# Decay-table rows spread over every sixteenth partition, and earlier products of zeros, in a fused RetNet and feed-forward kernel

**Chip, cores, metric.** One Trainium2 chip, one core. Times are device microseconds (us) of that core. Executions are compared with executions of the other kernel on the same chip.

## The reference

```python
# q, k, v: (4, 8, 768, 64); w_in: (512, 2048); w_out: (2048, 512); all f32
gamma = 1.0 - 2.0 ** (-5.0 - np.arange(H))
for t in range(S):
    state = gamma[None, :, None, None] * state + einsum('bhd,bhe->bhde', k[:, :, t], v[:, :, t])
    y[:, :, t] = scale * einsum('bhd,bhde->bhe', q[:, :, t], state)
x = y.transpose(0, 2, 1, 3).reshape(B * S, H * D)
h = x @ w_in
out = np.maximum(0.01 * h, h) @ w_out
```

The kernel does the recurrence in chunks of 128 tokens (scores, mask, products with the values, state) and the feed-forward part with seven block products in place of eight. Powers of the decay are needed per head and position; they come from a host-made table of 8 rows of 780 numbers, which three small matmuls spread over the 128 partitions.

## The kernel before

The change touches only the opening. In order of the program (cuts marked by `...`):

```python
x, t = xs[0]
rows = t[0:H, 1:3].rearrange("p i k n -> p (i k n)")[:, 0 : decay.shape[1]]
nc.scalar.dma_start(out=rows, in_=decay)         # the table: 8 rows, partitions 0 to 7
load_qk(0, 0); load_v(0, 0); load_qk(0, 1); ...  # SyncE's queue: all other loads
nc.vector.memset(mask, 1.0)
nc.gpsimd.affine_select(out=mask, ...)
...
nothing = t[:, 0, 0, :].bitcast(BF16)            # zeros, in the table's tile, other columns
nc.vector.memset(t[:, 0, 0, :], 0.0)

def keep_busy(n):                                # products of zeros
    for _ in range(n):
        nc.tensor.matmul(idle..., lhsT=nothing[:, 0:128], rhs=nothing, ...)
...
keep_busy(7)
score(0, 0)
nc.tensor.matmul(tables[:, 0, 0:H], lhsT=by_head, rhs=ones, ...)         # from the table
nc.tensor.matmul(tables[:, 0, H : H + HP], lhsT=place, rhs=g_c, ...)
masked(0, 0)
nc.vector.tensor_copy(out=dec[:, n_gq:], in_=tables[:, 0, 0 : H + HP])
nc.tensor.matmul(spread..., lhsT=place, rhs=g_q, ...)
nc.scalar.copy(out=dec[:, 0:n_gq], in_=spread...)
decay_v(0, 0, nc.vector)
score(0, 1)
values(0, 0)
```

## Time and profile before

| | before |
|---|---|
| median of 6 executions | 668.31 us (666.85 to 670.25) |
| profiled execution | 666.64 us, span 664.9 us |
| TensorE busy in the span | 659.4 us |
| first product of zeros / first scores / second scores start | 1.40 / 4.63 / 7.81 us |
| full clock from (the trace's record of the granted clock) | 6.01 us |
| first matmul of the hidden layer | 13.93 us |

A line of the timeline gives start, duration, engine, line, operation, written and read tile, number of records; in brackets the idle time before it and what ended that. `ap` are scores, `tables` and `spread` the products that make decay tables, `idle` the products of zeros, `d` the first hidden-layer products.

### The profile page before, as it was taken

To read this page: it belongs to the slowest core of one execution; us is meant where nothing else is said; L and a number is where in the kernel's file an instruction comes from. 1 tells how busy PE (TensorE), PEld (TensorE's weight loads), DVE (VectorE), ACT (ScalarE), POOL (GpSimd) and SP (SyncE) were. 2 spreads that over 40 slices of the span, in tenths; PEclk is the share of its full clock that TensorE was granted. 3 is DMA by queue.
4 is the path that set the end of the run, shared out by engine and by line. 5 is a ranking of instruction groups with operands and counts; after the bars stand their busy time and mean duration, and the time that the engine had idled before them with its cause. 6 is when DMAs were issued, how large, how long until landed. Compare 5 with 4: busy or idle time off the path is not lost.

```text
span 664.9 us, 10405 instructions
## 1 busy us (share of the span) xinstructions
PE 659.4 (99%) x4505; PEld 573.6 (86%) x4505; DVE 373.9 (56%) x570; ACT 175.8 (26%) x322; POOL 20.1 (3%) x22
## 2 busy tenths in 40 slices
PE   8999999999999999999999999999999999999998
PEld 5888888888888888888888888888888888888886
DVE  5789969889888676325543613663431444431342
ACT  5854555264261002212201311210221220221210
POOL 0000000000000111001000100100100000000000
PEclk9999999999999999999999999999999999999999
DMA  8920312313222453003012100301300001000001
GB/s 327 403 97 33 126 64 79 112 65 113 109 85 75 166 184 127 1 1 128 1 46 81 64 1 1 127 1 64 128 1 0 2 0 45 19 1 1 0 1 63
DMA packets 15758, 48.92 MB, mean 74 GB/s; under 512 B 1753, under 2 KB 2009, under 8 KB 15713
## 3 DMA queue, kind: packets, MB, share of 16 engines
q1 hardware_dynamic: 15696, 48.24, 20.1%
q8 instruction: 35, 0.57, 0.3%
q14 instruction: 11, 0.08, 0.0%
q10 hardware_dynamic: 16, 0.02, 0.0%
HBM read 41.97 MB, written 6.29 MB: 73 GB/s over the span
## 4 chain that ended last, share of the span: by engine, by line
PE 99%; DMA 1%; DVE 0%; issue 0%
PE B_o L414 13%; PE A_o L414 13%; PE C_o L414 12%; PE C_h L414 12%; PE B_h L414 12%; PE A_h L414 12%; PE D_o L414 6%; PE D_h L414 6%; PE ap L165 4%; PE yp L193 4%; PE d L436 2%; PE yp L184 2%; PE yp L208 1%; DMA qk<-in_qk_dram 1%; PE sums L208 0%; PE idle L626 0%
## 5 line engine op out<-in xcount | busy, mean ns | idle before, releaser
L414 PE MATMUL A_h<-x,w 128*128 128x256 f32 x368 | 87.0, 379 | 0.0
L414 PEld LDWEIGHTS A_h<-x,w 128*128 128x128 f32 x368 | 69.9, 190 | 9.6 <-issue 0.2
L414 PE MATMUL A_o<-g,w 128*128 128x256 f32 x288 | 68.0, 379 | 0.0
L449 ACT ACTIVATE g<-g 128x512 f32<-128x512 f32 x69 | 42.0, 630 | 92.4 <-DVE g L361 92.4
L414 PEld LDWEIGHTS A_o<-g,w 128*128 128x128 f32 x288 | 54.8, 190 | 7.4
L454 ACT COPY m<-A_h 128x512 f32<-128x512 f32 x23 | 13.4, 582 | 143.6 <-PE A_h L414 103.9
L361 DVE TENSOR_TENSOR m<-m,B_h 128x512 f32<-128x512 f32 x23 | 15.8, 686 | 55.5 <-PE B_h L414 55.5
L361 DVE TENSOR_TENSOR m<-m,B_o 128x512 f32<-128x512 f32 x16 | 11.0, 685 | 63.9 <-PE B_o L414 63.9
L238 DVE TENSOR_TENSOR x<-yp,dec 128x512 f32<-128x512 f32 x24 | 16.4, 689 | 49.7 <-PE yp L208 35.6
L414 PE MATMUL C_h<-t,w 128*128 128x256 f32 x184 | 44.1, 383 | 0.0
L414 PE MATMUL B_h<-x,w 128*128 128x256 f32 x184 | 44.1, 383 | 0.0
L414 PE MATMUL B_h<-t,w 128*128 128x256 f32 x184 | 43.5, 379 | 0.0
L414 PE MATMUL D_h<-t,w 128*128 128x256 f32 x184 | 43.5, 379 | 0.0
L414 PE MATMUL C_h<-x,w 128*128 128x256 f32 x184 | 43.5, 379 | 0.0
L414 PEld LDWEIGHTS C_h<-t,w 128*128 128x128 f32 x184 | 34.5, 190 | 5.5 <-issue 0.9
L414 PEld LDWEIGHTS B_h<-t,w 128*128 128x128 f32 x184 | 35.0, 190 | 4.7
L414 PEld LDWEIGHTS D_h<-t,w 128*128 128x128 f32 x184 | 35.0, 190 | 4.7
L414 PEld LDWEIGHTS C_h<-x,w 128*128 128x128 f32 x184 | 35.0, 190 | 4.7
L414 PEld LDWEIGHTS B_h<-x,w 128*128 128x128 f32 x184 | 34.5, 190 | 5.0 <-issue 0.3
L364 DVE TENSOR_TENSOR gd<-g,gd 128x512 f32<-128x512 f32 x48 | 37.1, 773 | 1.7
L170 DVE TENSOR_TENSOR am<-ap,mask 128x1024 f32<-128x1024 f32 x24 | 28.5, 1220 | 10.8 <-PE ap L165 10.8
L414 PE MATMUL B_o<-gd,w 128*128 128x256 f32 x144 | 34.0, 379 | 0.0
(118 smaller groups left out, 1019.0 us busy)
## 6 DMA issues: line engine op xcount, KB each, us to landing
raw<-in_weights_dram SPq DMA_DIRECT2D x31, 512.0 KB, 4.3
qk<-in_qk_dram SPq DMA_DIRECT2D x19, 512.0 KB, 3.8
kv<-in_kv_dram SPq DMA_DIRECT2D x17, 512.0 KB, 4.4
out_dram<-o SPq DMA_DIRECT2D x23, 256.0 KB, 2.1
in<-in_qk_dram SPq DMA_DIRECT2D x3, 512.0 KB, 8.7
in<-in_kv_dram SPq DMA_DIRECT2D x3, 512.0 KB, 8.5
kv<-in_kv_dram SPq DMA_DIRECT2D x4, 256.0 KB, 7.0
o_in<-in_qk_dram SPq DMA_DIRECT2D x2, 512.0 KB, 8.6
```

The costliest lines, as they stand in the source:

```text
L165: nc.tensor.matmul(ps[ts(u, 64), j, a, :], lhsT=x[ts(j, 64), 1, a, ts(u, 64)], rhs=x[ts(j, 64), 0, a, :])
L170: nc.vector.tensor_tensor(out=am.rearrange("p j a t -> p (j a) t"), in0=scores[c, b].rearrange("p j a t -> p (j a) t"), in1=mask.unsqueeze ...
L184: nc.tensor.matmul(ps[ts(i, 64), j, m, :], lhsT=st[b][ts(j, 64), a, :], rhs=x[ts(j, 64), 0, a, :], start=(m == 0), stop=False, skip_group_ ...
L193: nc.tensor.matmul(ps[ts(i, 64), j, m, :], lhsT=y[:, 1, 2 * a + j, :], rhs=am[:, j, a, :], start=(c == 0 and m == 0), stop=True, skip_grou ...
L208: nc.tensor.matmul(sp[ts(j, 64), a, :], lhsT=y[:, 0, 2 * a + j, :], rhs=y[:, 1, 2 * a + j, :], start=start, stop=True, skip_group_check=True)
L238: nc.vector.tensor_tensor(out=blocks, in0=ps[:, :, 0 : HP // 2, :], in1=gq, op=ALU.mult)
L361: nc.vector.tensor_tensor(out=out, in0=a, in1=b, op=ALU.add)
L364: nc.vector.tensor_tensor(out=out, in0=a, in1=b, op=ALU.subtract)
L414: nc.tensor.matmul(half, lhsT=block(w, sa)[:, k, ts(i, 128)], rhs=rhs[:, k, :], start=(first and (i == 0 or split) and n == 0 and k == 0), ...
L436: nc.tensor.matmul(banks[r][:, i, :], lhsT=block(2 * u, r + 2 * kh)[:, k, ts(i, 128)], rhs=x[:, 2 * kh + th, k, :], start=(step == 0 and i ...
L449: nc.scalar.activation(g[:, i], g[:, i], AF.Prelu, alpha=0.01)
L454: nc.scalar.copy(out=got["m1"], in_=ps)
```

## The change

Its intent: let the tables' products use the array's full height (rows in partitions 0, 16, 32, ... with zeros between), start the products of zeros sooner, and take two small pieces of work off VectorE.

```diff
-    rows = t[0:H, 1:3].rearrange("p i k n -> p (i k n)")[:, 0 : decay.shape[1]]
-    nc.scalar.dma_start(out=rows, in_=decay)
+    rows = t[:, 1:3].rearrange("p i k n -> p (i k n)")[:, 0 : decay.shape[1]]
+    nothing = t[:, 0, 0, 0:64].bitcast(BF16)
+    nc.vector.memset(t[:, 0, 0, 0:64], 0.0)
+    half = decay.shape[1] // 2
+    nc.gpsimd.memset(rows[:, :half], 0.0)
+    nc.vector.memset(rows[:, half:], 0.0)
+    nc.scalar.dma_start(out=rows[0 : 128 : 128 // H], in_=decay)
...
-    nothing = t[:, 0, 0, :].bitcast(BF16)
-    nc.vector.memset(t[:, 0, 0, :], 0.0)
...
-            nc.tensor.matmul(idle.rearrange("p i n -> p (i n)"), lhsT=nothing[:, 0:128],
-                             rhs=nothing, start=True, stop=True, skip_group_check=True)
+            nc.tensor.matmul(idle.rearrange("p i (two n) -> p (i two) n", two=2), lhsT=nothing,
+                             rhs=nothing.unsqueeze(1).to_broadcast([128, 4, 128]),
+                             start=True, stop=True, skip_group_check=True)
...
-    keep_busy(7)
+    keep_busy(8)
...
-    nc.vector.tensor_copy(out=dec[:, n_gq:], in_=tables[:, 0, 0 : H + HP])
+    nc.scalar.copy(out=dec[:, n_gq:], in_=tables[:, 0, 0 : H + HP])
...
-    decay_v(0, 0, nc.vector)
+    decay_v(0, 0)
```

## The prediction

> **What bounds the kernel now.** I read the page first, then the chain that ended last over the first 46 us, then the timeline of the first 15 us, because every line of the diff is executed in the opening. From the page:
>
> ```profile
> PE 659.4 (99%) x4505; PEld 573.6 (86%) x4505; DVE 373.9 (56%) x570; ACT 175.8 (26%) x322; POOL 20.1 (3%) x22
> PE 99%; DMA 1%; DVE 0%; issue 0%
> ```
>
> TensorE is busy for 659.4 of 664.9 us, so 5.5 us is all that removing its waits could give. The changed kernel has the same matmuls in the same order after the opening, so what it saves must come from TensorE's waits or its slow stretches before about 14 us. The chain by time shows that opening:
>
> ```profile
> 0.80 3.78 DMA qk<-in_qk_dram
> 4.59 0.04 issue
> 4.63 1.75 PE ap L165 x32
> 6.38 0.31 PE tables L638 x2
> 6.69 0.22 PE tables L640 x2
> 6.91 0.96 PE spread L644 x2
> 7.88 1.03 PE ap L165 x32
> 8.91 1.02 PE yp L193 x16
> ...
> 11.48 0.70 DVE x L238
> 12.18 0.05 issue
> 12.23 1.10 PE ap L165 x32
> 13.34 0.75 PE idle L626 x3
> 14.09 3.45 PE d L436 x16
> ```
>
> The first scores wait for the first transfer (4.59 us), whatever TensorE does before. The same 32 score records take 1.75 us the first time and 1.03 to 1.10 us later: their first six groups of four start 0.21 us apart, the later ones half of that. So TensorE runs at half rate until about 6.0 us, which agrees with the trace's record of the clock: full from 6.01 us. The slow stretch costs 1.75 - 1.10 = 0.65 us here. The timeline has the rest:
>
> ```profile
> 0.80 0.58 ACTq L592 DMA_DIRECT2D t<-decay_dram  x1
> 0.90 0.17 DVE L609 MEMSET mask<- 128x128 f32 x1 [0.90 <-PEq L836]
> 1.07 0.27 DVE L621 MEMSET t<- 128x256 f32 x1
> 1.40 3.17 PE L626 MATMUL idle<-t 128*128 128x512 bf16 x7 [1.40 <-DVE t L621]
> 7.67 0.16 DVE L643 COPY dec<-tables 128x12 f32<-128x12 f32 x1
> 7.87 0.69 DVE L147 TENSOR_TENSOR kv<-kv,dec 128x512 f32<-128x512 f32 x1
> 8.39 1.07 POOL L147 TENSOR_TENSOR kv<-kv,dec 128x512 f32<-128x512 f32 x1 [6.96 <-DMA kv<-in_kv_dram]
> 8.98 1.23 DVE L170 TENSOR_TENSOR am<-ap,mask 128x1024 f32<-128x1024 f32 x1 [0.42 <-PE ap L165]
> ```
>
> The products of zeros exist only to keep TensorE active; they start at 1.40, when VectorE has cleared their operand.
>
> **What the Trainium skill says.** "TensorE: Matmul & The Clock Gate", Part 1: TensorE starts at 1.2 GHz and is let up to 2.4 GHz after a sustained busy window of about 3.4 us; the window runs free of the kernel's start, so the moment varies from run to run. The trace agrees on the rates: the idle products' weight loads are 0.425 us apart (512 columns at 1.2 GHz), and the later products of the same form take about 0.21. Its full clock came 6.01 - 1.40 = 4.61 us after the first product, between one and two windows. The same page, "LDWEIGHTS (loading the stationary operand)": a load's time goes by columns, not by rows of contraction. The trace agrees: 187 ns for the 8-row loads of the tables, 190 ns for 128-row loads of f32. So full-height tables cost TensorE no more time. "SBUF — State Buffer", "SBUF: two separate sides": VectorE and GpSimd exclude each other only where VectorE uses the shared port pair, for example with two operands in SBUF. The masking reads PSUM and one SBUF operand; it took 1.23 us with GpSimd at work beside it (8.98) and 1.22 to 1.23 elsewhere, so a second GpSimd product does not slow it.
>
> **The change part by part.**
> 1. *Zeros sooner.* The memset of 64 columns is now VectorE's first. From 0.17 us for 128 columns and 0.27 for 256, a column costs 0.78 ns and the fixed part is 0.07 us: 64 columns take 0.12 us. TensorE starts at 0.90 + 0.12 + 0.05 (the lag seen before) = 1.07 instead of 1.40, so 0.33 us sooner. Eight products fill 8 x 0.425 = 3.40 us, to 4.47; seven from 1.40 filled to 4.38. Both end before the transfer at 4.59, so the eighth costs nothing. What is gained is an earlier window: on average 0.33 us less at half rate. Where that stretch falls on work, it is worth half, some 0.16 us.
> 2. *Clearing before the transfer.* The table's transfer now waits for two memsets of 390 columns. VectorE's takes 0.07 + 390 x 0.78 ns = 0.37 us and is done at 1.40. For GpSimd I have only its 128-column select of 0.29 us, so at worst 0.9 us from 0.8, done at 1.7. The issue moves from 0.80 to between 1.45 and 1.75. In the trace its eight packets of 3,120 B were all done by 2.43, 1.63 us after the issue; now that is 3.1 to 3.4, perhaps 4 because it shares the engines with the first load. The tables are wanted at about 6. Off the path. The 24 KB now run beside the 512 KB of the first scores' load: 5% of it, at most about 0.1 us on the 4.59.
> 3. *Full-height tables.* The same four pairs of records, the same columns: 0 us of TensorE time. Its effect can only be on how activity is counted (rival A).
> 4. *Copy to ScalarE, first decay to GpSimd.* VectorE loses 0.16 + 0.69 = 0.85 us of work, but then waits for the second scores, which end at 8.91: its next masking stays at 8.98. On the other side, the 12-column copy need no longer wait behind the masking (6.53 to 7.76): ScalarE does it at about 6.95 to 7.2, GpSimd's product takes 1.07 us, done at about 8.3; the products with the values want it at 8.84. GpSimd is free again before the second values land (8.39). Nothing gained, nothing lost.
> 5. *How much of an earlier TensorE reaches the end.* In the trace the second scores' load had landed at 7.59 and they began at 7.81, 0.07 before the modelled end of the table product, which is how TensorE passes from group to group: TensorE was the bound, by about 0.2 us. The third scores began at 12.23; their load landed at 12.10, and the tile before was taken at 12.17. So of any gain, about 0.1 us survives to 12.2 when the clock comes as in this trace. Sum: 0.33 x 0.5 = 0.16, capped at about 0.1, less up to 0.1 for the shared transfer: 0 to 0.1 us of 668.
>
> **The rivals.**
> A. *The window is missed in many runs of before.* If eight-row products hardly count as activity, a window that holds the tables (6.3 to 7.8) fails and the full clock comes 3.4 us later, which costs up to 3.4 x 0.5 = 1.7 us of work. For it: the profiled execution took 666.64, while the median is 668.31 and the slowest 670.25; the first step is 1.67 us. Full-height rows and an earlier start would bring most runs to 666.5 to 667. Against it: the one trace shows no missed window, and the spread can have other causes, such as the transfers that run near 400 GB/s from 5 to 25 us.
> B. *The transfers bound the opening anyway.* For it: landing and need lie within 0.2 us at both 7.8 and 12.2, and the queue is saturated. The time would stay at 668.0 to 668.4.
> C. *A new wait takes the old one's place.* If GpSimd's memset or the shared queue makes the table late, the tables stand in TensorE's order ahead of the second scores, and every tenth is lost directly; if GpSimd's first decay comes late, so do the values' products. Against it: slack of 2 us on the first, 0.5 us on the second. It would make 669 to 670.
>
> **Range and chances.** I weigh A at 0.4 with 666.9, B and the bare sum at 0.45 with 668.2, C at 0.15 with 669.2: 0.4 x 666.9 + 0.45 x 668.2 + 0.15 x 669.2 = 667.8. The range, 666.4 to 669.3, is wider than the sum because three runs of the kernel before already span 3.4 us. A change of 2% is 13.4 us, the whole opening, so the chances of that are token: faster 0.01, same 0.98, slower 0.01.
>
> **What would show each step right or wrong.** Step 1: the first idle product at about 1.07 and eight of them, the scores still at about 4.6. Step 2: the table product never waits for its transfer. Step 3: the table loads still at about 187 ns, now of 128 rows. Step 4: the copy on ScalarE near 7.0, GpSimd's first decay done before 8.5, VectorE's second masking within 0.2 us of 8.98. Step 5: third scores no earlier than about 12.1 and the chain from 14 us on unchanged. A: the full clock's start spread by one window or more between executions of before and not of after, and after's times tighter. I am wrong if the opening up to the first hidden-layer product (13.9 us) moves by over 1 us without a change of clock, if anything after 46 us changes, or if the median leaves the range.

## The result, and the profile after

The changed kernel took 672.74 us (median of 6, 671.79 to 673.46) against 668.31: ratio 1.0063, 95% interval 1.0041 to 1.0086. That is within 2%, but clearly slower, and above the predicted range of 666.4 to 669.3. A ratio here and below is the mean time of one kernel's fast executions over that of the other's of the same rounds, so not quite the ratio of the medians. A repetition beside the experiments gave 672.29 us, ratio 1.0073 (1.0058 to 1.0088).

The busy line of the page of the changed kernel shows the same TensorE work in a span of 670.4 us:

```profile
PE 659.3 (98%) x4506; PEld 572.5 (85%) x4506; DVE 371.6 (55%) x569; ACT 175.7 (26%) x323; POOL 21.1 (3%) x24
```

So 5.5 us of waiting were added between these two executions (that of before, 666.64 us, was among its fastest; the medians differ by 4.4). Where: busy times by stretch, first the kernel before, then the changed one (stretch, its length, then busy us of each engine with instructions, the clock, the DMA share and GB/s).

```profile
0.00:5.00 5.00, 3.54 (x15) 1.26 (x19) 0.44 (x2) 1.28 (x1) 0.50 (x5) 1.00 0.52 174
5.00:10.00 5.00, 5.00 (x87) 3.69 (x79) 3.01 (x4) 1.04 (x2) 1.07 (x1) 1.00 0.96 378
```

```profile
0.00:5.00 5.00, 0.00 (x0) 0.00 (x0) 0.64 (x3) 1.28 (x1) 0.92 (x6) 1.00 0.58 181
5.00:10.00 5.00, 2.55 (x7) 0.93 (x8) 0.00 (x0) 0.00 (x0) 0.00 (x0) 1.00 1.01 398
```

TensorE did nothing in the first 5 us. The 1.00 in the clock's column does not show the start: the record begins only where the full clock does. The timeline of the changed kernel tells what TensorE waited for:

```profile
0.89 0.11 DVE L593 MEMSET t<- 128x64 f32 x1 [0.89 <-PEq L841]
...
1.50 1.17 ACTq L597 DMA_DIRECT2D t<-decay_dram  x1
...
7.45 3.44 PE L629 MATMUL idle<-t 128*128 128x512 bf16 x8 [7.45 <-DMA t<-decay_dram]
```

VectorE has the zeros ready at 1.00 us, but the products of zeros start at 7.45, released by the table's transfer, although they read no column of the table. In the trace two waits for semaphores (counters that tell an engine when another has finished) stand before the first product: an instruction of the products' own line waits for the semaphore of the table's transfer, then the first weight load waits for VectorE's. In the kernel before, there is VectorE's alone. The memsets of the rows (VectorE 1.03 to 1.41, GpSimd 0.80 to 1.22) come ahead of that transfer, which is issued at 1.50 instead of 0.80 and needs 5.81 us instead of some 2 until it lands, that is, until its last completion is recorded. (SyncE's next load of weights also waits 1.9 us for that landing and is issued at 7.33 instead of 5.55; the chain to the end contains no transfer but the table's.) The chain of the changed kernel (start, duration, what):

```profile
1.50 5.81 DMA t<-decay_dram
...
7.45 3.44 PE idle L629 x8
10.89 1.03 PE ap L165 x32
...
13.42 1.03 PE ap L165 x32
...
19.17 3.86 PE d L436 x16
```

The eight products of zeros, which used to fill a wait, now stand on the path: the first scores start at 10.82 instead of 4.63, although their load had landed at 4.6. The first hidden-layer product is at 19.17 instead of 13.93, and the 5.24 us between are nearly the whole 5.5. The scores now run at full rate (1.10 instead of 1.75 us), which gives 0.65 of the 6.19 us back.

### The profile page after: what moved, and what is told of

The parts are those of the page before. It is cut to its first block, busy times and chain, and to the rows that moved or that the text cites. A ratio compares the mean times of both kernels' runs of the same rounds, so it can differ in the third digit from the quotient of the medians.

```text
span 670.4 us, 10409 instructions
## 1 busy us (share of the span) xinstructions
PE 659.3 (98%) x4506; PEld 572.5 (85%) x4506; DVE 371.6 (55%) x569; ACT 175.7 (26%) x323; POOL 21.1 (3%) x24
## 4 chain that ended last, share of the span: by engine, by line
PE 98%; DMA 1%; DVE 0%; issue 0%; DVEq 0%
PE B_o L414 12%; PE A_o L414 12%; PE C_o L414 12%; PE C_h L414 12%; PE B_h L414 12%; PE A_h L414 12%; PE D_o L414 6%; PE D_h L414 6%; PE yp L193 3%; PE ap L165 3%; PE d L436 2%; PE yp L184 2%; PE yp L208 1%; DMA t<-decay_dram 1%; PE idle L629 1%; PE sums L208 0%
## 5 line engine op out<-in xcount | busy, mean ns | idle before, releaser
L364 DVE TENSOR_TENSOR gd<-g,gd 128x512 f32<-128x512 f32 x48 | 35.4, 737 | 1.7
L147 POOL TENSOR_TENSOR kv<-kv,dec 128x512 f32<-128x512 f32 x18 | 20.2, 1125 | 463.3 <-DMA kv<-in_kv_dram 258.8
```

Source lines behind the costliest of these rows:

```text
L147: engine.tensor_tensor(out=v, in0=v, in1=gk.unsqueeze(2).to_broadcast([128, H, D]), op=ALU.mult)
L364: nc.vector.tensor_tensor(out=out, in0=a, in1=b, op=ALU.subtract)
```

## The experiments

Theory W: the wait of the products of zeros for the table costs the time. Rivals: L, the late table alone costs it; M, the moves to ScalarE and GpSimd cost it. Of each kernel six executions were compared with eleven of the kernel before on the same chip.

| run | median (us) | range (us) | ratio to before, 95% |
|---|---|---|---|
| a1 changed, again | 672.29 | 671.85 to 672.73 | 1.0073, 1.0058 to 1.0088 |
| e1 zeros in another tile | 668.41 | 667.56 to 671.02 | 1.0026, 1.0005 to 1.0048 |
| e2 rows together | 667.10 | 666.66 to 667.77 | 1.0001, 0.9984 to 1.0017 |
| e2 again | 666.87 | 666.65 to 667.00 | 0.9990, 0.9975 to 1.0005 |
| e3 before, table late | 668.87 | 666.38 to 670.66 | 1.0020, 0.9994 to 1.0045 |
| e4 no zeros | 670.24 | 669.68 to 670.67 | 1.0045, 1.0030 to 1.0060 |
| e5 moves only | 667.64 | 667.06 to 670.28 | 1.0009, 0.9988 to 1.0029 |
| e6 e1, table second in queue | 667.52 | 666.92 to 667.89 | 1.0003, 0.9988 to 1.0019 |
| e7 wait kept, table early | 671.31 | 670.78 to 671.74 | 1.0058, 1.0043 to 1.0072 |
| e8 e6 with 8 rows | 667.47 | 666.84 to 668.98 | 1.0000, 0.9982 to 1.0018 |
| e9 e1, wait filled | 668.17 | 667.46 to 668.73 | 1.0009, 0.9993 to 1.0024 |

The kernel before had medians of 666.95 or 666.96 on these chips.

**a1: the changed kernel once more**, on the chip of e3, e5 and e7; no edit.

> The changed kernel unaltered, on the chip of this job, to have it beside the experiments. 1.005 to 1.009 of the kernel before, first product of zeros again at 7 to 7.5 us, none of its runs as short as the kernel before.

As expected: the slowdown is there again, and the first product of zeros is at 7.10 us:

```profile
7.10 3.57 PE L629 MATMUL idle<-t 128*128 128x512 bf16 x8 [7.10 <-DMA t<-decay_dram]
```

**e1: the changed kernel without the false wait.**

```diff
-    nothing = t[:, 0, 0, 0:64].bitcast(BF16)
-    nc.vector.memset(t[:, 0, 0, 0:64], 0.0)
+    parts = [new_g(0, 0)]                  # moved up; its difference tile is not used yet
+    zeros = parts[0][2][:, 0, 0, 0:64]
+    nothing = zeros.bitcast(BF16)
+    nc.vector.memset(zeros, 0.0)
```

> The changed kernel with the zeros in another tile, so that the products of zeros no longer wait for the table's transfer; all else as changed. Theory W (that wait is the cost): first product of zeros at 1.1 us instead of 7.4, first scores at 4.6; the tables then still wait for a transfer that lands near 7.3, so the second scores start near 8.8 instead of 7.8 (before) or 13.4 (changed); about 668.0 to 669.5 us. Rival L (the late table, not the wait, is the cost): zeros early, but the time stays within 1 us of the changed kernel's 672.7. Rival M (the moves to ScalarE and GpSimd cost it): also stays near 672.7.

Most of the loss is gone. Timeline of e1, profiled in an execution of 669.13 us:

```profile
1.05 3.22 PE L630 MATMUL idle<-gd 128*128 128x512 bf16 x8 [1.05 <-DVE gd L595]
...
6.95 0.36 PE L644 MATMUL tables<-t 128*128 128x8 f32 x2 [1.23 <-DMA t<-decay_dram]
...
7.59 2.05 PE L650 MATMUL spread<-t 128*128 128x512 f32 x2
...
9.58 1.57 PE L165 MATMUL ap<-qk 64*64 64x128 f32 x32
```

Zeros at 1.05 and, in the same view, first scores at 4.62, as W expected. The tables then wait 1.23 us for the transfer, and `spread` takes 2.05 us instead of 1.10: the clock fell. The record of the clock says full from 3.76, half from 7.18, full again from 10.59 us. The second scores start at 9.58, later than the 8.8 expected, for this reason. Of the six executions three took 667.6 to 667.7 and three 669.1 to 671.0. The recorded clock of the three slow ones, as a mean over the span, is 0.997, 0.995 and 0.995, that of the others 0.999 to 1.000; one window of 3.41 us at half rate is 0.003 of the span, so the slow ones fell for one or two windows.

**e2: rows together in partitions 0 to 7, no clearing, transfer at once; zeros sooner and moves kept.**

```diff
-    rows = t[:, 1:3].rearrange("p i k n -> p (i k n)")[:, 0 : decay.shape[1]]
+    rows = t[0:H, 1:3].rearrange("p i k n -> p (i k n)")[:, 0 : decay.shape[1]]
-    half = decay.shape[1] // 2
-    nc.gpsimd.memset(rows[:, :half], 0.0)
-    nc.vector.memset(rows[:, half:], 0.0)
-    nc.scalar.dma_start(out=rows[0 : 128 : 128 // H], in_=decay)
+    nc.scalar.dma_start(out=rows, in_=decay)
```

> The changed kernel with the table's eight rows in partitions 0 to 7 as before, without the clearing, so its transfer is issued at 0.8 us and nothing else waits for it; the zeros sooner and the moves to ScalarE and GpSimd stay. Theories W and L both: transfer landed by 2.5 us, first product of zeros at 1.1, opening as before or up to 0.3 us sooner, 667 to 668.5 us. Rival M (the moves cost it): stays above 671.

As expected, but for the landing at 2.67 us instead of by 2.5, for which nothing waits. Timeline of e2:

```profile
1.05 3.59 PE L626 MATMUL idle<-t 128*128 128x512 bf16 x8 [1.05 <-DVE t L593]
...
6.41 0.17 ACT L645 COPY dec<-tables 128x12 f32<-128x12 f32 x1 [3.73 <-PE tables L642]
6.67 1.04 POOL L147 TENSOR_TENSOR kv<-kv,dec 128x512 f32<-128x512 f32 x1 [5.16 <-ACT dec L645]
```

The zeros lie in the table's tile here too, and the trace has no wait for the transfer before them. Nor has e3 below, which keeps the clearing (of 8 rows) and not the stride: the wait comes with the strided rows. That the framework's tracking takes a destination of every sixteenth partition as covering the columns between is inferred from the waits in these traces; its code was not read. Rival M falls: with both moves in place GpSimd's product is done at 7.71, well before the values' products.

**e4: the changed kernel without the first products of zeros**.

```diff
-    keep_busy(8)
+    keep_busy(0)
     score(0, 0)
```

> The changed kernel without the first eight products of zeros, so nothing stands before the first scores; the late table stays. Theory W: the first scores start at 4.6 us at half rate, the tables wait for the transfer to land near 7.3, the clock stays low until about 8 to 12 us; 3 to 4.5 us faster than the changed kernel, 668.2 to 669.7, so that the products meant to help cost more than they give. Rival L: within 1 us of 672.7.

Timeline of e4, first scores, `spread` and second scores:

```profile
4.81 1.98 PE L165 MATMUL ap<-qk 64*64 64x128 f32 x32 [4.81 <-DMA qk<-in_qk_dram]
...
8.15 2.05 PE L649 MATMUL spread<-t 128*128 128x512 f32 x2
...
10.13 1.99 PE L165 MATMUL ap<-qk 64*64 64x128 f32 x32
```

The scores start at 4.81 and the tables wait for the transfer until 7.30, but the full clock comes only at 12.25 us, so tables and second scores take nearly twice their time. The gain over the changed kernel is 0.0073 - 0.0045 = 0.0028, some 1.9 us, less than the 3 to 4.5 expected: dropping the products saves their place on the path and loses the clock.

**e6: e1 with the table's transfer second in SyncE's queue.**

```diff
-    nc.scalar.dma_start(out=rows[0 : 128 : 128 // H], in_=decay)
     load_qk(0, 0)
+    nc.sync.dma_start(out=rows[0 : 128 : 128 // H], in_=decay)
```

> As e1_zeros_own_tile, and the table's transfer is issued on SyncE's queue right after the first scores' load, ahead of all others, instead of on ScalarE's queue. Theory W with the table queued behind other loads: landed between 4.0 and 5.5 us instead of 7.3, the tables don't wait, second scores at 7.7 to 8.1; 667 to 668.5 us, 0.5 to 1 below e1. If the strided rows themselves make the transfer slow: lands near 7 as before and no faster than e1. If full-height tables matter for the clock: tighter times than the kernel before, mean below 667.5.

Timeline of e6, the table's issue, the tables and the second scores (the first scores start at 4.38):

```profile
1.50 0.72 SPq L600 DMA_DIRECT2D t<-decay_dram  x1
...
5.42 0.39 PE L644 MATMUL tables<-t 128*128 128x8 f32 x2
...
7.84 1.10 PE L165 MATMUL ap<-qk 64*64 64x128 f32 x32 [0.85 <-DMA qk<-in_qk_dram]
```

The table's last completion is recorded at 5.04 us, the tables wait for nothing, and the kernel is level with before. So full height itself shows no cost (the interval allows up to 0.2%) and no gain in the times of six executions: none was below 666.9.

**e7: the wait kept, the table early** (e6's queue, zeros in the table's tile as changed; against the changed kernel).

```diff
-    nc.scalar.dma_start(out=rows[0 : 128 : 128 // H], in_=decay)
     load_qk(0, 0)
+    nc.sync.dma_start(out=rows[0 : 128 : 128 // H], in_=decay)
```

> A smaller dose of the same wait: the zeros stay in the table's tile, so the products of zeros wait for its transfer, but that is issued second in SyncE's queue and lands near 4 us (it did in e6). Theory W: first product of zeros near 4.2 us, eight of them take 3.4 us, first scores at 7.6 to 7.8 instead of 4.4 (e6) and 10.8 (changed), 1.5 to 3 us above e6, so 1.002 to 1.005 of the kernel before. If the wait did not matter (rival L), as e6, 1.000.

Chain of e7:

```profile
1.50 3.93 DMA t<-decay_dram
...
5.57 3.57 PE idle L629 x8
```

The transfer landed at 5.43, not near 4: I had taken the packets' start in e6 for their landing. So the loss against e6 is also larger than the 1.5 to 3 us expected. The zeros start at 5.57, 4.5 us after e6's 1.05, and the ratio is 0.0055 above e6, 3.7 us. In a1 they start at 7.10, 6.05 us after e6's, and the ratio is 0.0070 above it, 4.7 us. Both are about 0.8 us of time for each us that the zeros wait: the cost follows the dose (in a1 the table's queue differs from e6's as well), and rival L, which expected e7 to equal e6, falls.

**e3: the kernel before with only the memsets ahead of the table's transfer.**

```diff
+    nc.gpsimd.memset(rows[:, :half], 0.0)      # rows: partitions 0 to 7
+    nc.vector.memset(rows[:, half:], 0.0)
     nc.scalar.dma_start(out=rows, in_=decay)
```

> The kernel before with its eight rows in partitions 0 to 7, and only the two memsets ahead of the table's transfer, so that it is issued near 1.5 to 2 us behind the other loads: late table alone, no stride, no false wait. If being late in the queue is the cause of the late landing: lands at 6.5 to 7.5 us as in the changed kernel and in e1, the tables wait until then, 1.001 to 1.004 of the kernel before, and in some runs the clock falls while TensorE waits. If the stride over partitions were the cause: lands by 4 us, 1.000.

A miss with a lesson. The issue took 0.58 us at 1.42, the last completion is at 5.25 us, between the two forecasts, and the tables did not wait. Yet three executions took 670.6 and three 666.4 to 667.2. The profiled one is a slow one, its full clock came at 14.36 us, and TensorE's timeline shows what comes before it at half rate, scores in 1.99 and `spread` in 2.05 us:

```profile
1.80 3.17 PE L629 MATMUL idle<-t 128*128 128x512 bf16 x7 [1.80 <-DVE t L624]
4.90 1.99 PE L165 MATMUL ap<-qk 64*64 64x128 f32 x32
...
7.69 2.05 PE L647 MATMUL spread<-t 8*128 8x512 f32 x2
```

The memset of the zeros came third on VectorE, so the products of zeros started 0.4 us later than before (1.80, not 1.40). Nothing else that TensorE waits for had moved, so this is the likely cause that three of six executions, and not five of 39, fell into the slow group. The trace supports it: counted back from 14.36 in steps of 3.413 us (the spacing of the clock's changes in e1, e5 and e8), a window ends at 4.12, of which products of zeros from 1.80 on fill 2.32 us. TensorE was busy for 2.66 us of the window after which e5 got the full clock, and for 2.71 us of e1's.

**e9: e1 with the wait filled.** Five more products of zeros after the first scores.

```diff
     keep_busy(8)
     score(0, 0)
+    keep_busy(5)
```

> As e1_zeros_own_tile (strided rows, late table, no false wait) with five more products of zeros after the first scores, which fill the wait for the table. If half of e1's runs were slow because the clock fell in that wait: no fall in the trace, six runs between 667.2 and 668.3, ratio 1.001 to 1.002 that is left for the wait itself. If the clock had no part in it: the same two groups of times as e1 (667.6 and 669 to 671).

Timeline of TensorE in e9:

```profile
6.26 1.25 PE L630 MATMUL idle<-gd 128*128 128x512 bf16 x5
7.92 0.36 PE L645 MATMUL tables<-t 128*128 128x8 f32 x2 [0.41 <-DMA t<-decay_dram]
...
8.36 1.10 PE L651 MATMUL spread<-t 128*128 128x512 f32 x2
```

The transfer landed later still here (7.79 us), yet the clock stayed full from 5.95 us on, `spread` kept its 1.10 us, and no execution exceeded 668.73 (668.3 was expected). The recorded clock of all six is 0.999 to 1.000. e1's slow group is gone. Six executions without it could be chance, but the recorded clock of e1's own executions says the same: a falling clock made the slow ones slow.

**e5: the moves alone**, in the kernel before (the last two pairs of lines of the change's diff).

> The kernel before with only the 12-column copy on ScalarE and the first decay product on GpSimd. Theories W and L: no change, 0.999 to 1.001. Rival M (a slower engine becomes the wait): the products with the values start later than 8.84 us and 1.001 to 1.005.

Timeline of TensorE in e5:

```profile
6.25 1.10 PE L644 MATMUL spread<-t 8*128 8x512 f32 x2
7.29 1.86 PE L165 MATMUL ap<-qk 64*64 64x128 f32 x32
```

The ratio's interval includes 1. The profiled execution (667.68 us) had its clock fall from 7.47 to 10.89 us, so the second scores took 1.86 us and the products with the values came at 9.08, later than the 8.84 that rival M named as its sign. They stand right behind those scores, though, and e2, with the same moves and no fall, has them at 8.52. The run does not speak for M; a loss of up to 0.3% by the moves alone is not excluded by it.

**e8: e6 with the eight rows together**, to test the height of the tables' products at the same timing.

```diff
-    rows = t[:, 1:3].rearrange("p i k n -> p (i k n)")[:, 0 : decay.shape[1]]
+    rows = t[0:H, 1:3].rearrange("p i k n -> p (i k n)")[:, 0 : decay.shape[1]]
...
-    nc.sync.dma_start(out=rows[0 : 128 : 128 // H], in_=decay)
+    nc.sync.dma_start(out=rows, in_=decay)
```

> As e6_table_second_in_queue but with the eight rows together in partitions 0 to 7 (the memsets stay ahead of the transfer), so that only the height of the tables' products and the stride of the transfer differ from e6. If products of 8 rows count less than full ones for the clock: the trace or some of the six runs show a fall or a late start of the full clock, runs some 1.5 to 3.5 us above the best, where e6 had none. If not: as e6, 667.0 to 668.0 in all runs. The issue should take near 0.4 us instead of 0.72 if the stride makes it longer, and the table land at or before 5.0 us.

Two of six executions took 668.8 and 669.0, and the trace of one shows the clock falling from 8.24 to 11.65 us. But in that execution the second scores also waited 1.30 us for their load, against 0.85 in e6's trace, so height and wait are mixed: not settled. The recorded clock is 0.997 in these two executions and 0.999 to 1.000 in the other four; in e6 it is 1.000 in all six. The stride's part is clear: the issue takes 0.36 us here and 0.72 in e6, and the table lands at 4.22 instead of 5.04.

**e2 again**, for the spread.

> e2_rows_together once more, to see whether it has the slow runs near 670.2 that the kernel before shows in some of its runs. If the earlier start of the products of zeros makes the clock's start safer: no run above 668.5 in six more. If not: one or two near 670. Ratio 0.998 to 1.000.

No execution above 667.0; with the first six, none of twelve above 667.8. The kernel before had 5 of 39 between 670.06 and 670.25. At that rate twelve without one would happen by chance about one time in five, and the ratio's interval includes 1: e2 is the version to keep, equal to the kernel before, with a smaller spread that is possible and not shown.

## Why the prediction was wrong

Step by step, as it put them:

1. *"TensorE starts at 0.90 + 0.12 + 0.05 = 1.07 instead of 1.40"*: **this is the step that failed.** The memset did take 0.11 us and was done at 1.00, and where nothing else is waited for (e1, e2, e6) the start is at 1.05. In the changed kernel it is 7.45, because the products had gained a wait for the table's transfer. The wait is an instruction of the program, so a look at the program's waits could have told it; I had read which instructions moved, and not the waits of that line. e1 takes that wait away and the ratio goes from 1.0073 to 1.0026, which makes it 3.1 us of the 4.9; e7 shows the cost following the dose. The prediction's own sign of being wrong came as well: the first hidden-layer product moved by 5.24 us.
2. *"now that is 3.1 to 3.4, perhaps 4 ... Off the path"*: wrong by 3.3 to 4.2 us, against 7.31. The issue came at 1.50, as forecast. I carried over the 1.63 us from the issue to the end of the last packet, of a transfer that was first in line; its last completion came 2.02 us after the issue. Two terms were missing beside that, with the last completions recorded in the traces: 2.82 us when issued first (before), 5.25 when issued at 1.42 behind other loads (e3), 6.8 to 7.8 when strided as well (e1, a1 and the changed kernel, e4, e9). With the false wait gone, the late table still makes the tables wait about 1.2 us (e1), and the clock may fall in that wait. This is the likely place of the rest of the loss, 1.8 us of the 4.9: with the table early (e6) or the wait filled (e9) the ratio is 1.0003 or 1.0009, though their intervals overlap with e1's.
3. *Full-height tables cost nothing*: right. At the full clock, loads of 128 rows took 186 to 192 ns, those of 8 rows 181 to 188; e6 is level within its interval.
4. *The moves*: right where they could be seen undisturbed: in e2 the copy at 6.41, GpSimd done at 7.71, the second masking at 8.66.
5. *"about 0.1 us survives"*: could not apply to the changed kernel. e2, the change without the strided rows, measured 1.0001 and 0.9990, which does not contradict a sum of 0 to 0.1 us for that kernel and is too coarse to confirm it.

**The rivals.** C named "a new wait takes the old one's place", with the table late in TensorE's order, at 15% and 669 to 670. The kind was right, but I placed it at the tables (with "slack of 2 us") and not at the products of zeros, so even C was 3 us short. A had a true core: executions of the kernel before span 3.4 to 3.7 us in each job, and e3's slow execution shows the full clock at 14.36 us. That a late start explains before's five slow executions is inferred, since none of them was traced; the recorded clock, which does not show the start, is 1.000 in the three for which it is listed. Between them and the fast ones I overlooked a third group: six of the 33 executions beside the experiments took 667.6 to 668.1 at a recorded clock of 0.997, as e5's traced execution did, whose clock fell for one window. A's forecast that the changed kernel's times are tighter holds as well (0.9 us of range in a1, against 3.5 of before in the same rounds), but at the high level: the late products of zeros are followed by dense work, and the clock is full at 10.62 and 11.28 us in its two traces, about when the scores start.

**Still open.** It is open whether products of 8 rows hold the clock less well than full ones (e5 and e8 fell, e6 did not, but with different waits). The wait alone does not tell them apart: TensorE was busy for 3.04 of the 3.41 us before e5's fall, and in e6 for only 2.86 of the 3.41 us that followed its full clock, after which the clock stayed. Over all runs the recorded clock is 0.997 in 11 of 63 executions with tables of 8 rows (before 6 of 33, e2 1 of 12, e5 and e8 2 of 6 each, e3 none of 6) and in none of the 12 of e6 and e9; at that rate none of 12 has a chance of about 10%. This leans towards rival A's premise and does not show it. Open too is why a strided destination takes twice as long to issue.

## What to carry to other kernels

After changing where a transfer writes, compare the waits of every instruction that reads the same tile, not only the order of instructions: a strided destination can make the framework see an overlap that is not there, and the cure is to keep unrelated data in another tile. A transfer's time from issue to landing belongs to its place among the loads, so 0.6 us later at the issue was 2.4 us later at the landing (e3), and 0.7 us later with the stride 4.5 us (the changed kernel). Filler work is free only while it waits for nothing itself.

## What the Trainium skill lacked or had wrong

- "TensorE: Matmul & The Clock Gate", "Why this matters for your kernels", advises no TensorE-idle gaps above about 3 us between bursts of matmuls. In e1 the clock fell after a wait of 1.23 us (with 0.35 us more idle before it in the same window), in e5 after a window with 0.37 us idle in all; in e9, with e1's wait mostly filled, it did not. The page has no figure for such short gaps. The window is as Part 1 of the page has it: the changes in e1's record are at 3.76, 7.18 and 10.59 us, 3.413 us apart. It also has the full clock after at least one busy window: in e3 TensorE was busy in all of the two windows of 3.41 us that end at 7.53 and 10.95, and the full clock came only at 14.36. How much a product of few rows counts as busy (these windows hold 64-row score tiles and 8-row products) the page does not say, and no run here separates it.
- "DMA: Bandwidth & Descriptors", "Queues, rings and completion order", says that the engines take turns between queues packet by packet, which would let 24 KB pass. Issued at 1.50 us on a queue of its own, its first packet started at 5.72 us, after the 512 KB and 256 KB issued before it had landed (last completion 5.22); issued at 0.80, its first packet started at 1.73. In e3 it started at 4.13, before those two loads had landed (4.62 and 5.43). Whether the packets waited behind others or were made late, no trace here tells, so this is a gap and not a contradiction. The page has no cost of a stride over partitions at the issue either: 1.17 us against 0.58 on ScalarE's queue, 0.72 against 0.36 on SyncE's, for the same 8 rows.
